# Attention beside a state-space scan on one core: input loaded in two token halves, first head group split by keys, rotation tables grown from 128 tokens

## The chip, the cores and the metric

The kernel runs on one core of a Trainium2 chip. The core has a matrix engine (TensorE: PE for its matmuls, PEld for its weight loads), a vector engine (VectorE, DVE), a scalar engine that evaluates functions (ScalarE, ACT), a general-purpose engine (GpSimd, POOL) and an engine that here only issues DMAs (SyncE, SP). Each engine runs its own list of instructions in order, and semaphores make one wait for another. The metric is the time of one execution on the device in microseconds (us), as the median of several runs.

## The reference

Two independent computations share the output, columns 0 to 639 and 640 to 1279 of a 2048-token sequence. The first (A) is a complex diagonal recurrence along the tokens, the second (B) is attention with 32 query heads that share one key and one value head of width 20.

```python
Lam_bar = exp(exp(log_dt) * Lam);  B_bar = ((Lam_bar - 1) / Lam)[:, None] * Bmat
Bu = einsum("bld,pd->blp", x, B_bar)
h = Lam_bar * h + Bu[:, t]                       # for t in 0..2047
y = 2 * einsum("bld,dp->bld", hseq, Cmat).real + x * Dskip

q = (x @ wq).reshape(1, 2048, 32, 20);  k = x @ wk;  v = x @ wv
p = softmax(einsum("bhqd,bkd->bhqk", q, k) * 20**-0.5)
b = einsum("bhqk,bkd->bhqd", p, v).reshape(1, 2048, 640) @ wo
out = concatenate([y, b], axis=-1)
```

## The kernel before, in words

The attention bounds the work. It is cut into 32 groups: 4 blocks of 512 queries times 8 groups of 4 heads. A group has 64 units, one for each of its 4 heads and each of 16 chunks of 128 keys; there are 2048 units. For a unit PE multiplies keys (`KT`) with queries (`QT`), which gives 128 x 512 scores in PSUM. Most units are then exponentiated on ACT, in tiles of three or two units (`ex_op`, P<-R, 128x1536 or 128x1024, line 1295). The rest ("D units") go to DVE, which makes an integer approximation of the exponential in one pass out of PSUM (line 1301) and three shifted copies from it in passes over several units (line 1307). PE multiplies the results with the values (`VP`) and sums a group in one PSUM bank, `PV`; a column of ones in `VP` gives the softmax denominators. When a group is complete, DVE copies `PV` to `OTr` (line 1343), from where it goes to memory, is normalized and multiplied with `wo`.

The scores need a bound that keeps the exponential in range. The row `mabs` holds the largest absolute key over all tokens for each of the 20 features; PE multiplies its table (`Mblk`) with the absolute queries and subtracts the product from the queries' scores by way of a constant key row (row 20 of each head in `KT`). This is called the guard. It needs the keys of all 2048 tokens before the first score.

The scan A turns the recurrence into a real one by rotating with cosine and sine tables `cs` of 5 x 512 columns, which `tables` builds in the set-up: three DVE passes and two ACT passes (lines 711 to 719) for each of 5 channel blocks. The DVE scan (line 957), products on POOL (line 945) and matmuls follow, spread over the whole run.

What sets the order: `setup` emits its instructions in the order in which they are written, then `main` runs a planner at build time. The planner has a list of threads (deques of operations), estimates when each operation could start, and appends the one that could start first, with small biases and some noise from a table of seeds, to its engine's list. So the order on every engine is fixed when the kernel is built, and an engine that waits holds up everything behind the wait. A thread named `rest` holds the end of the set-up (key copies, value products); while it is not empty, no PV product is offered, and not more than about half of the first group is filled.

In the set-up of before, SP issues six transposing DMAs for the attention's input `xbT` (four with 2048 tokens, the last channel block in two halves), PE forms all keys in four PSUM banks as the channel blocks arrive, DVE takes the largest absolute keys (line 574), ACT copies half of the keys to `KT` (line 565), and the guard follows.

Of the kernel before, what the change touches and what calls it, by code (L numbers as in the profile page):

```python
# [254 lines left out]
class _Kernel:  # L255
# [15 lines left out]
    SPIN = 1, 0, 5, 2  # L271
# [5 lines left out]
    SEEDS = (19, 1987, 2263, 3089, 4041, 5474, 6444, 7290, 8492, 9186, 10683, 11194, 12742, 13024, 14829,  # L277
# [33 lines left out]
    def alloc(self):  # L311
# [32 lines left out]
        self.sb("E1", [128, 4], BF16)  # L344
# [3 lines left out]
        self.tri = self.Pd[:].rearrange("p s u n -> p (s u n)").bitcast(FP32).rearrange("p (r n) -> p r n", n=512)  # L348
# [5 lines left out]
        self.wq_raw = self.P[:].rearrange("p s n -> p (s n)")[:, 18 * 512:18 * 512 + NC * 640].rearrange("p (c n) -> p c n", c=NC)  # L354
# [14 lines left out]
        self.sb("CGim", [128, NC, 640], BF16)  # L369
        self.sb("DiagD", [128, NC, 128], BF16)  # L370
        self.sb("sv", [128, 4, NC], FP32)
        self.sb("sc", [128, 24, NC], FP32)
        self.sb("ang", [128, 3, 4, NC], FP32)
        self.sb("rot", [128, 4, NC], FP32)
# [3 lines left out]
        self.sb("tm", [128, 8, 512], BF16)  # L378
        self.ctmp = self.tm[:].rearrange("p i n -> p (i n)").bitcast(FP32)[:, 1024:1664]
# [19 lines left out]
    def go(self, o):  # L399
        r, w = o.keys()  # L400
        occ = o.occ * self.pace(self.p.begin("pe", r, w, o.accum)) if o.eng == "pe" else o.occ
# [55 lines left out]
    def setup(self):  # L457
        t, NC, S = self.t, self.NC, self.S
        self.x_keys = [f"xbT{c}" for c in range(NC)] + [f"xbT{NC - 1}b"]
# [10 lines left out]
        go(self.dma(K.wk_raw, t["wk"].rearrange("(c p) n -> p c n", p=128), "wk", writes=["wk_raw"], kb=25, q="act"))  # L470
        go(self.dma(K.wq0, t["wq"][:, 0:80].rearrange("(c p) n -> p c n", p=128), "wq0", writes=["ostage0"], kb=100, q="act"))
        go(self.dma(K.wv_raw, t["wv"].rearrange("(c p) n -> p c n", p=128), "wv", writes=["wv_raw"], kb=25))
# [9 lines left out]

        pool(lambda e: e.memset(K.ident[:], 0.0), writes=["ident"])
# [5 lines left out]
        pool(lambda e: e.iota(K.iota_i, pattern=[[1, 512]], base=0, channel_multiplier=0), writes=["hh1"], occ=0.6)  # L489
        pool(lambda e: e.tensor_copy(K.iota_f, K.iota_i), reads=["hh1"], writes=["hh0"], occ=0.6)  # L490
        pool(lambda e: e.memset(K.wk4, 0.0), writes=["wk4"], occ=0.6)
# [4 lines left out]
        pool(lambda e: e.memset(K.wq0p, 0.0), writes=["ystage"], occ=0.6)  # L496
        dve(lambda e: e.memset(K.half[:], 1.0), writes=["half"], n=3)
        for j in range(4):
            dve(lambda e, j=j: e.memset(K.half[32 * j:32 * j + 32, 1 - j % 2:2 - j % 2], 0.0), ["half"], ["half"], n=1)

# [8 lines left out]
        pk = ["P7", "P8", "P9"]  # L509
        go(self.dma(K.wq_raw, t["wq"].rearrange("(c p) n -> p c n", p=128), "wq", writes=["wq_raw"] + pk, kb=800))  # L510
        pad = lambda x: x.rearrange("p c (j r) -> p c j r", r=32)[:, :, :, 0:20]
# [5 lines left out]
        for pat, base, cm, cmp in (([[0, 4], [1, 32]], -20, 0, ALU.is_equal),  # L517
# [4 lines left out]
                reads=mk, writes=mk, occ=0.4)  # L522
        pool(lambda e: e.memset(K.wq1[:], 0.0), writes=["wq1"], occ=0.6)
        pool(lambda e: e.memset(K.OTr[:, 1, :], 0.0), writes=["OTr1"], occ=0.6)

        self.tables(dve, act, {
            1: lambda: act(lambda e: e.activation(pad(K.wq0p), K.wq0.rearrange("p c (j r) -> p c j r", r=20), ACT.Copy),
                           ["ostage0", "ystage"], ["ystage"], n=400),
            3: turn})
        act(lambda e: e.activation(K.half[:, 2:3], K.half_pi[:], ACT.Exp), ["half_pi", "half"], ["half2"], n=1)  # L530


        banks = [(K.R[1], 0, "R1"), (K.R[1], 512, "R1b"), (K.BB, 0, "B0"), (K.BB, 512, "B1")]
        for bt, off, key in banks:
            go(self.mms([self.m1(bt[:, off:off + 512], K.selrow[:, :], K.onesrow[:, :], True, False)],
                        ["selrow", "onesrow"], [key], accum=True))
# [14 lines left out]
        for c in range(NC - 1):  # L551
            k_part(c, range(4))
            spin((0, 0, self.SPIN[0], 0)[c])
# [1015 lines left out]
```

## Time and profile before

| | |
|---|---|
| median of 3 runs | 756.54 us (755.94 to 757.65) |
| the profiled execution | 756.86 us, its span 755.1 us |
| ACT busy | 740.4 us (98%) |
| DVE busy | 711.0 us (94%) |
| PE busy | 699.2 us (93%) |
| POOL busy | 349.3 us (46%) |
| first exponential on ACT starts | 21.08 us |

The span reaches from the first to the last instruction. Busy times are unions: where two records of an engine overlap, the time counts once. A line of a timeline gives start, length, engine, source line, operation, output <- input, count, and in brackets the idle time before it with what ended it. A line of instruction groups gives the shapes, the count, busy time and the mean length of one in ns.

### The profile page before, as it was taken

How to read it: one execution, taken by the hardware profiler on the slowest of the kernel's cores; microseconds unless marked ns; L12 is line 12 of the kernel's file. 1: busy time of each engine (PE TensorE's matmuls, PEld its weight loads, DVE VectorE, ACT ScalarE, POOL GpSimd, SP SyncE). 2: the span in 40 equal slices, each digit the busy share in tenths (PEclk: the TensorE clock that was granted, in tenths of full speed). 3: DMA queues.
4: the chain of work that ended last, by engine and by line, in shares of the span. 5: the costliest groups of instructions: out<-in, count | busy, mean ns of one | idle time of the engine just before them, and what ended most of it. 6: DMA issues, size and time to landing. Idle time of an engine off the chain costs nothing.

```text
span 755.1 us, 22636 instructions
## 1 busy us (share of the span) xinstructions
PE 699.2 (93%) x9643; PEld 225.0 (30%) x9643; DVE 711.0 (94%) x1108; ACT 740.4 (98%) x712; POOL 349.3 (46%) x708
## 2 busy tenths in 40 slices
PE   5899987889999999999999999999999999989997
PEld 2222222222222333322223333222233332223334
DVE  6599999999998999999999899999999999999986
ACT  8999999999999999999999999999999999999995
POOL 5702344479975000287683201577722443882040
PEclk9799999999999999999899999999999999999999
DMA  9377301000020003200002002200000211000021
GB/s 191 66 128 155 68 16 50 8 25 16 4 58 16 33 19 76 68 11 16 15 10 70 26 25 77 60 8 18 8 25 20 69 42 40 1 16 17 21 62 37
DMA packets 61202, 31.89 MB, mean 42 GB/s; under 512 B 41510, under 2 KB 61102, under 8 KB 61102
## 3 DMA queue, kind: packets, MB, share of 16 engines
q1 hardware_dynamic: 59606, 30.14, 16.3%
q8 instruction: 77, 1.26, 0.7%
q10 hardware_dynamic: 1496, 0.30, 0.2%
q14 instruction: 23, 0.19, 0.1%
HBM read 9.21 MB, written 12.69 MB: 29 GB/s over the span
## 4 chain that ended last, share of the span: by engine, by line
ACT 63%; PE 21%; DVE 14%; issue 1%; POOL 1%; ACTq 0%; DVEq 0%
ACT P L1295 61%; PE R L448 7%; PE PV L448 7%; PE B L448 7%; DVE Pd L1307 5%; DVE Pd L1301 5%; DVE hh L957 2%; DVE tm L929 1%; ACT cs L719 0%; ACT KT L565 0%; DVE ostage L1089 0%; DVE OTr L1343 0%; ACT Pd L718 0%; DVE Qd L803 0%; ACTq L421 0%
## 5 line engine op out<-in xcount | busy, mean ns | idle before, releaser
L1295 ACT ACTIVATE P<-R 128x1024 bf16<-128x1024 f32 (+1 forms) x679 | 721.0, 1296 | 3.7 <-PE R L448 1.7
L448 PE MATMUL R<-QT,KT 32*128 32x512 bf16 (+1 forms) x1686 | 267.6, 389 | 36.6 <-ACT P L1295 26.6
L448 PE MATMUL PV<-Pd,VP 128*32 128x512 bf16 x1860 | 271.2, 385 | 4.0 <-DVE Pd L1307 1.7
L448 PE MATMUL PV<-P,VP 128*32 128x512 bf16 x1583 | 265.5, 389 | 0.4
L1301 DVE TENSOR_SCALAR Pd<-B 128x512 int16<-128x512 f32 x362 | 243.8, 681 | 15.4 <-PE B L448 13.1
L1307 DVE TENSOR_SCALAR Pd<-Pd 128x1536 int16<-128x1536 int16 (+3 forms) x356 | 250.0, 709 | 2.8
L945 POOL TENSOR_TENSOR tm<-hh,cs 128x128 bf16<-128x128 f32 x320 | 161.1, 528 | 162.9 <-DVE hh L957 153.5
L448 PEld LDWEIGHTS R<-QT,KT 32*128 32x128 bf16 (+1 forms) x1686 | 67.0, 91 | 294.2 <-ACT P L1295 264.5
L448 PE MATMUL B<-QT,KT 32*128 32x512 bf16 x362 | 140.0, 387 | 0.0
L945 POOL TENSOR_TENSOR W<-tm 128x128 bf16<-128x128 bf16 x160 | 79.9, 523 | 37.2 <-PE B L448 33.0
L448 PEld LDWEIGHTS PV<-Pd,VP 128*32 128x32 bf16 x1860 | 65.7, 94 | 70.3 <-issue 41.9
L448 PEld LDWEIGHTS PV<-P,VP 128*32 128x32 bf16 x1583 | 63.6, 94 | 51.3 <-issue 39.6
L1301 DVE TENSOR_SCALAR Pd<-R 128x512 int16<-128x512 f32 x103 | 69.9, 678 | 1.3 <-PE R L448 1.0
L1039 POOL TENSOR_TENSOR OTd<-OTd,rwide 128x128 bf16<-128x128 bf16 x80 | 34.2, 455 | 72.9 <-DMA OTd<-o_rows 71.0
L886 POOL TENSOR_SCALAR tm<-W,sc 128x128 f32<-128x128 bf16 x40 | 30.0, 765 | 63.9 <-DMA W<-in_A_C_im_dram 26.6
L929 DVE TENSOR_TENSOR tm<-B,cs 128x1024 bf16<-128x1024 f32 x40 | 48.6, 1214 | 1.1 <-PE B L448 0.9
L448 PE MATMUL B<-CGre,W 128*32 128x384 bf16 (+1 forms) x640 | 47.7, 304 | 0.0
L448 PE MATMUL B<-CGim,W 128*32 128x384 bf16 (+1 forms) x640 | 46.9, 299 | 0.0
L957 DVE TENSOR_TENSOR_SCAN hh<-sc,hini,B 128x512 f32<-128x512 f32 x30 | 38.0, 1270 | 0.0
L448 PEld LDWEIGHTS B<-QT,KT 32*128 32x128 bf16 x362 | 32.8, 91 | 0.5 <-DVE ystage L990 0.3
L448 PE MATMUL B<-xaT,BTre 128*32 128x512 bf16 x400 | 32.3, 383 | 0.5 <-DVE hh L957 0.3
L448 PE MATMUL B<-xaT,BTim 128*32 128x512 bf16 x400 | 32.3, 395 | 0.5 <-DVE tm L929 0.2
(153 smaller groups left out, 438.4 us busy)
## 6 DMA issues: line engine op xcount, KB each, us to landing
o_rows<-OTr SPq DMA_DIRECT2D x32, 128.0 KB, 1.7
QT<-q_rows SPq DMA_DIRECT2D x30, 128.0 KB, 2.2
q_rows<-Qd SPq DMA_DIRECT2D x16, 160.0 KB, 2.9
OTd<-o_rows SPq DMA_DIRECT2D x16, 160.0 KB, 3.3
out_dram<-ystage SPq DMA_DIRECT2D x16, 160.0 KB, 1.8
out_dram<-ostage SPq DMA_DIRECT2D x12, 160.0 KB, 1.8
P<-in_B_wq_dram SPq DMA_DIRECT2D x1, 800.0 KB, 5.2
WO<-in_B_wo_dram SPq DMA_DIRECT2D x4, 200.0 KB, 3.6
```

The lines of the kernel that those rows point to most:

```text
L448: ins = e.matmul(o() if callable(o) else o, lhsT=l, rhs=r, start=st, stop=sp, skip_group_check=True, **kw)
L886: pool(lambda e, y=y, c=c, gy=gy, i=i: e.tensor_scalar(K.ctmp[:, i:i + 128], y[:, i:i + 128], sc[:, gy, c:c + 1], None, op0=ALU.mult), key ...
L929: dve(lambda e, k=k, h=h: e.tensor_tensor(K.tm[:, 2 * k:2 * k + 2, :], bass.AP(tensor=K.BB, offset=512 * int(h.key[1]), ap=[[512 * self.BA ...
L945: put(lambda e, c0=c0, end=end: e.tensor_tensor(out[:, c0:end], a[:, c0:end], b[:, c0:end], op), reads, [writes + h], n, gate=None if i el ...
L957: dve(lambda e, ri=ri, ini=ini, h=h: e.tensor_tensor_scan(K.hh[:, ri, :], dec, h.T[:, :], ini, ALU.mult, ALU.add), ["sc", None, "hini"], [ ...
L1039: ops.append(Op("pool", lambda e, c=c, m=m: e.tensor_tensor(K.OTd[:, m, c], K.OTd[:, m, c], K.rwide[:, c], ALU.mult), rw + [f"OTe{dd}" for ...
L1295: return Op("act", lambda e: e.activation(dst, K.R[n % 2][:, 0:512 * size], ACT.Exp, scale=self.exp_scale), [f"R{n % 2}"] + ["R0c"] * (siz ...
L1301: return Op("dve", lambda e: e.tensor_scalar(K.Pd[:, 0, u, :], K.B[x][:, :], self.d_off, 0.0, op0=ALU.add, op1=ALU.max), [key], [f"Pd{u}_0 ...
L1307: return Op("dve", lambda e: e.tensor_scalar(K.Pd[:, i:i + n, a:b, :].rearrange("p s u n -> p s (u n)"), K.Pd[:, 0:n, a:b, :].rearrange("p ...
```

## The change

Four things are changed together, and a new table of seeds comes with them.

1. **Two token halves.** `xbT` is loaded by ten transposing DMAs of 1024 tokens, first all five channel blocks of tokens 0 to 1023, then those of 1024 to 2047. In `setup` PE forms the keys of the first half only, in the two banks `B0` and `B1`. The second half's keys are in `rest`, and the value products, one operation for each half and channel block (8 small matmuls), in a new thread `vals`.
2. **First head group split by keys.** Group 0 becomes two blocks: block -1 over key chunks 0 to 7 and block 0 over key chunks 8 to 15, with 32 units each. Block -1 uses queries `QT3` whose guard comes from the first half's keys. `rest` then forms the guard of all keys, the queries `QT0` that use it (PE adds the difference of the two guards to `QT3`, then one DVE copy), and a factor `frac`, the exponential of the difference of the two guards (8 matmuls with `E1`, one ACT pass of 128x512). When block -1 is complete, DVE multiplies its `PV` with the factor into `early`; when block 0 is complete, DVE adds `early` to its `PV`. `frac` and `early` lie in `OTd`, which is not used that early.
3. **Tables grown.** `tables` builds cosine and sine for tokens 0 to 127 of all five channel blocks in one go (four DVE passes and one ACT pass over 128x640, one ACT pass over 128x1280). The other 384 columns are rotations of them: for each of 5 channel blocks, 3 steps and 2 tables, one POOL product (`growth`, a multiplication with a per-partition scalar, 128x128 in 32-bit floats) and one DVE operation that multiplies and adds, 30 of each. The DVE ones are in a thread `grow`. No D unit is taken for block -1, nor while `rest` or `grow` is not empty.
4. **Set-up in the scheduler.** The threads `rest`, `vals`, `loads` (inputs of the scan), `grow` and `guard` (the small DMAs of `mabs`) are all given to the planner. The raw `wq` moves from the ring `P` to `CGre`. The load of `wv` moves from SP to ACT's queue. PE's filler products, which add zeros to `PV` where PE would be idle, read `xbT` in place of `cs`.

The orders of the instructions around three places follow, before and then after. First, ACT from the last table of the set-up to the first exponential; `sv` are per-channel constants, `sc` the decay, `Qabs` the absolute queries of the guard.

```order
L701 ACTIVATE rot<-ang 128x20
L718 ACTIVATE Pd<-Pd,quarter 128x512
L719 ACTIVATE cs<-Pd,half_pi 128x1024
L530 ACT_TABLE_LOAD
L530 ACTIVATE half<-half_pi 128x1
L579 ACTIVATE sv<-R 128x5 x2
L581 ACTIVATE Qabs<-PV 128x512
L565 ACTIVATE KT<-R,half 128x512 x4
L594 ACTIVATE sc<-sc 128x5
L1295 ACTIVATE P<-R 128x1536
```

```order
L521 ACTIVATE WO<-WO 128x5x20 x4
L758 ACTIVATE Pd<-Pd,quarter 128x640
L759 ACTIVATE tm<-Pd,half_pi 128x1280
L743 ACTIVATE rot<-ang 128x50
L573 ACTIVATE sv<-R 128x5 x2
L574 ACT_TABLE_LOAD
L574 ACTIVATE half<-half_pi 128x1
L577 ACTIVATE sc<-sc 128x5
L600 ACTIVATE Qabs<-R 128x512
L586 ACTIVATE KT<-B,half 128x512 x4
L1362 ACTIVATE P<-R 128x1536
```

The two table passes for each of five channel blocks have become two passes in all, and the constants `sv` and the decay stand ahead of the guard's queries.

Second, DVE from the first queries `QT` onward.

```order
L786 TENSOR_SCALAR QT<-PV 128x512
L596 TENSOR_TENSOR mabs<-mabs 128x1
L569 TENSOR_SCALAR KT<-B,half 128x512 x4
L602 MEMSET VP 128x1024
L603 MEMSET VP 128x16 x4
L605 TENSOR_SCALAR VP<-PV 128x16x20 x4
```

```order
L846 TENSOR_SCALAR QT<-R 128x512
L763 CAST cs<-tm 128x10x128
L781 SCALAR_TENSOR_TENSOR cs<-tm,rot,Pd 128x128 x19
L632 TENSOR_SCALAR VP<-PV 128x16x20 x4
L617 TENSOR_TENSOR mabs<-mabs 128x1
L638 TENSOR_REDUCE mabs<-B 128x1
L617 TENSOR_TENSOR mabs<-mabs 128x1 x2
L590 TENSOR_SCALAR KT<-B,half 128x512 x2
L643 TENSOR_SCALAR Mblk<-Pd,mabs 128x128
L781 SCALAR_TENSOR_TENSOR cs<-tm,rot,Pd 128x128 x4
L630 CAST QT<-B 128x512
```

A cast and 19 of the 30 growth operations now stand between the first queries and the values `VP`, and the second half's guard behind those. On POOL the 30 products of the growth stand directly behind the product for the decay:

```order
L593 TENSOR_TENSOR sc<-sc,sv 128x5
L611 COPY wqd<-P 128x640 x5
L614 TENSOR_SCALAR nident<-ident 128x128
L650 MEMSET Md 128x160
L652 AFFINE_SELECT Md<-Md 128x160 x4
```

```order
L576 TENSOR_TENSOR sc<-sc,sv 128x5
L779 TENSOR_SCALAR Pd<-tm,rot 128x128 x30
L688 MEMSET Md 128x160
L690 AFFINE_SELECT Md<-Md 128x160 x4
L656 COPY wqd<-CGre 128x640 x5
```

The copies `wqd`, the weights from which the queries of groups 2 to 7 are made, have moved behind the 30 products.

Third, PE after the value products, in the stretch in which ACT works on its first tiles (R are the tiles of scores).

```order
L448 MATMUL PV<-WO,xbT 128x20 x20
L448 MATMUL R<-QT,KT 128x512 x7
L448 MATMUL PV<-P,VP 32x512 x8
L448 MATMUL R<-QT,KT 128x512 x3
L448 MATMUL PV<-P,VP 32x512 x4
```

```order
L453 MATMUL R<-QT,KT 128x512 x2
L453 MATMUL PV<-P,VP 32x512 x4
L453 MATMUL B<-QT,ident 128x512
L453 MATMUL B<-Qabs,Mblk 128x512
L453 MATMUL R<-QT,KT 128x512 x3
L453 MATMUL PV<-xbT,VP 32x512 x4
L453 MATMUL R<-QT,KT 128x512 x2
L453 MATMUL PV<-P,VP 32x512 x4
L453 MATMUL B<-QT,E 32x512 x8
```

PE now forms the second queries (`B<-QT,ident` and `B<-Qabs,Mblk`) ahead of the scores of the eleventh tile, and the factor's exponent (`B<-QT,E`) ahead of those of the thirteenth.

Over the whole program ACT has 445 exponentials of 1024 and 232 of 1536 columns where it had 454 and 225, DVE has 462 D units where it had 465, and PE has 160 filler products where it had 100.

The diff, cut to its core:

```diff
-        for c in range(NC):
-            for t0, n, key in (((0, S, f"xbT{c}"),) if c < NC - 1 else ((0, S // 2, f"xbT{c}"), (S // 2, S // 2, f"xbT{c}b"))):
-                go(self.dma(K.xbT[:, c, t0:t0 + n], t["xb"][0, t0:t0 + n, 128 * c:128 * (c + 1)], key, writes=[key], tr=True,
-                            kb=n // 4))
+        for i, h in enumerate("ab"):
+            for c in range(NC):
+                key, t0 = f"xbT{c}{h}", 1024 * i
+                go(self.dma(K.xbT[:, c, t0:t0 + 1024], t["xb"][0, t0:t0 + 1024, 128 * c:128 * (c + 1)], key, writes=[key],
+                            tr=True, kb=256))
...
+        go(ones(0))
+        go(ones(1))
+        for c in range(NC):
+            for tb in range(2):
+                go(k_mm(c, tb))
+            if c < 2:
+                spin(self.SPIN[0])
+            elif c == 2:
+                for o in blk[:3]:
+                    go(o)
+                go(self.mms([self.m1(K.R[1][:, 0:10], K.vecD, K.ident[0:10, 0:10], True, True)], ["ident", "veclre", "vecdsk"], ["R1"]))
...
+        self.rest = deque([
+            ones(2), ones(3), *(k_mm(c, tb) for c in range(NC) for tb in (2, 3)),
+            small(3, 0, 1, ALU.max, ["mabs0", "mabs1"]),
+            Op("dve", lambda e: e.tensor_reduce(out=mcol(2), in_=K.BB[:, 0:1024], axis=AX.X, op=ALU.max,
+                                                apply_absolute_value=True), ["B0", "B1"], ["mabs2"], occ=dve_t(1024)),
+            top,
+            small(3, 4, 3, ALU.subtract, ["mabs4", "mabs3"]),
+            *copy("dve", 2),
+            Op("dve", lambda e: e.tensor_scalar(K.Mblk[:], K.mask, mcol(3), self.c1, op0=ALU.mult, op1=ALU.mult), mk + ["mabs3"], ["Mblk"],
+               occ=dve_t(128)),
+            *again, *last,
...
+            self.mms(diff, ["E1", "QT0", f"QT{self.QRING - 1}"], ["B0"], kind="C"),
+            Op("act", lambda e: e.activation(K.frac, K.B[0][:, :], ACT.Exp, scale=self.exp_scale), ["B0"], self.frac_keys,
+               occ=act_t(512), lat=0.12),
...
+    def growth(self, pool):
+        K, NC, grow = self, self.NC, self.grow
         for c in range(NC):
+            for k in (1, 2, 3):
+                for i in range(2):
+                    m = 2 * (3 * c + k - 1) + i
+                    tmp, tk = K.flat[:, 4608 + 128 * m:4736 + 128 * m], f"gt{m}"
+                    s, co = K.rot[:, 2 * k, c:c + 1], K.rot[:, 2 * k + 1, c:c + 1]
+                    pool(lambda e, c=c, i=i, s=s, tmp=tmp: e.tensor_scalar(tmp, K.base[:, 1 - i, c, :], s, None, op0=ALU.mult),
+                         self.base_keys + ["rot"], [tk], 0.385)
+                    grow.append(Op("dve", lambda e, c=c, i=i, co=co, tmp=tmp, k=k: e.scalar_tensor_tensor(
+                        out=K.cs[:, c, i, 128 * k:128 * k + 128], in0=K.base[:, i, c, :], scalar=co, in1=tmp, op0=ALU.mult,
+                        op1=(ALU.subtract, ALU.add)[i]), self.base_keys + ["rot", tk] + self.row_keys(9 + m // 4),
+                        [f"cs{c}{i}{k}"], occ=dve_t(128)))
...
-        qt_done = self.qt_done = {0}
+        qt_done = self.qt_done = {-1}
+        half_kc = self.NKC // 2
+        blocks = [range(half_kc, self.NKC)] + [range(self.NKC)] * (NG - 1) + [range(half_kc)]
...
-            if not (g > 0 or taken[g] >= 24) or d_group(g) is None:
+            if g < 0 or rest or self.grow or d_group(g) is None:
                 return False
...
+            if g < 0:
+                return Op("dve", lambda e: e.tensor_tensor(K.early, K.PV[:, :], K.frac, ALU.mult), ["PV"] + K.frac_keys, K.early_keys,
+                          occ=dve_t(512))
+            if g == 0:
+                return Op("dve", lambda e: e.tensor_tensor(K.OTr[:, sl, :], K.PV[:, :], K.early, ALU.add), ["PV"] + K.early_keys,
+                          [f"OTr{sl}"], occ=dve_t(512))
```

More of the change, by code (lines that the diff above doesn't have):

```diff
@@ L585, in setup @@
                 go(o)
-        last = bass.AP(tensor=K.mabs, offset=1, ap=[[5, 128], [0, 128]])
-        dve(lambda e: e.scalar_tensor_tensor(out=K.Mblk[:], in0=last, scalar=K.mabs[:, 0:1], in1=K.mask, op0=ALU.max,
+        dve(lambda e: e.scalar_tensor_tensor(out=K.Mblk[:], in0=wide(1), scalar=mcol(0), in1=K.mask, op0=ALU.max,
                                              op1=ALU.mult), mk + ["mabs0", "mabs1"], ["Mblk"], n=128)
+        spin(self.SPIN[1])
+        va = [self.v_part(0, c) for c in range(NC)]
@@ new lines, in setup @@
+        top = small(4, 2, 3, ALU.max, ["mabs2", "mabs3"])
+        top.done = lambda: self.max_done.add(0)
+        last = list(copy("dve", 3))
+        last[-1].done = lambda: self.qt_done.add(0)
+        self.max_done = set()
+        diff = [self.m1(K.B[0][32 * j:32 * j + 32, :], bass.AP(tensor=K.E1, offset=4 * i + j, ap=[[8, 128], [0, 32]]),
+                        K.QT[:, r, :], i == 0, i == 1, (0, 32 * j), 4) for i, r in ((0, 0), (1, self.QRING - 1)) for j in range(4)]
+        q1, q2 = K.QT[:, self.QRING - 1, :], K.QT[:, 0, :]
@@ L1352, in main @@
             cand = []
-            if half and not any(x[1][0] == half[0][1][0] for x in dunits) and taken[half[0][1][0]] > self.DLAST:
+            if half and not any(x[1][0] == half[0][1][0] for x in dunits) and late(half[0][1][0]):
                 shifts.extend((tuple(half), x) for x in self.PASSES)
@@ L1361, in main @@
             t_fill = None
-            early = bool(rest) and any(self.NKC - len(x) >= 8 for x in left[0])
-            if cur["fill"] < cur["act"] + 2 and any(x < 64 for x in taken) and not early:
+            if cur["fill"] < cur["act"] + 2 and taken != size_of:
                 n = cur["fill"]
-                g = next(i for i in range(NG) if taken[i] < 64)
+                g = next(i for i in groups if taken[i] < size_of[i])
                 if g in qt_done:
```

319 lines of the change are left out of this document (167 added, 152 removed), and 8 rows, old and new, of the table SEEDS.

## The prediction

> **What bounds the kernel now.** I read the page's busy times and chain first, then the windows and waits of ACT, then the timeline of the set-up, since the change is made there.
>
> ```profile
> span 755.1 us, 22636 instructions
> ACT 63%; PE 21%; DVE 14%; issue 1%; POOL 1%; ACTq 0%; DVEq 0%
> 21.00:100.00 79.00, 74.39 (x938) 22.24 (x938) 70.41 (x123) 78.13 (x75) 28.59 (x57) 0.94 0.54 101
> 100.00:745.00 645.00, 606.17 (x8484) 193.86 (x8482) 624.13 (x952) 642.14 (x608) 308.53 (x622) 0.99 0.11 30
> 745.00:755.10 10.10, 6.32 (x190) 4.52 (x180) 3.28 (x6) 2.27 (x3) 0.00 (x0) 0.93 0.20 68
> L1295 ACT ACTIVATE P<-R 128x1024 bf16<-128x1024 f32 (+1 forms) x679 | 721.0, 1296 | 3.7 <-PE R L448 1.7
> ...
> L1295 ACT ACTIVATE P<-R 128x1024 bf16<-128x1024 f32 x454 | 473.7, 1152 | 1.9 <-PE B L448 0.9 <-PE R L448 0.6
> L1295 ACT ACTIVATE P<-R 128x1536 bf16<-128x1536 f32 x225 | 357.2, 1588 | 1.8 <-PE R L448 1.1 <-PE B L448 0.4
> ```
>
> In a window's row the fourth busy time is ACT's: it is idle for 0.87 us from 21 to 100 and for 2.86 us from 100 to 745. So between the first exponential and the tail ACT is full, and the time is: start of the first exponential, plus ACT's work, plus a few us of idle, plus a tail of ten. The chain's 14% on DVE warn that DVE (624.13 of 645, 96.8%) is nearly as full. Before the first exponential the timeline of ACT reads:
>
> ```profile
> 1.68 0.41 ACTq L421 DMA_DIRECT2D WO<-in_B_wk_dram  x1
> ...
> 4.36 1.28 ACT L503 ACT_TABLE_LOAD   x1
> 5.96 1.24 ACT L507 ACTIVATE WO<-WO 128x100 bf16<-128x100 bf16 x4
> ...
> 14.81 0.70 ACT L718 ACTIVATE Pd<-Pd,quarter 128x512 f32<-128x512 f32 x1
> 15.55 1.15 ACT L719 ACTIVATE cs<-Pd,half_pi 128x1024 bf16<-128x1024 f32 x1
> 16.72 1.28 ACT L530 ACT_TABLE_LOAD   x1
> 18.01 0.20 ACT L530 ACTIVATE half<-half_pi 128x1 f32<-128x1 f32 x1
> 18.12 0.22 ACT L579 ACTIVATE sv<-R 128x5 f32<-128x5 f32 x2
> 18.23 0.60 ACT L581 ACTIVATE Qabs<-PV 128x512 f32<-128x512 f32 x1
> 18.71 2.44 ACT L565 ACTIVATE KT<-R,half 128x512 bf16<-128x512 f32 x4
> 20.99 0.25 ACT L594 ACTIVATE sc<-sc 128x5 f32<-128x5 f32 x1
> 21.08 2.41 ACT L1295 ACTIVATE P<-R 128x1536 bf16<-128x1536 f32 x2
> ```
>
> ACT hardly pauses: the ten table passes (7 to 16.7) hold up the first exponential as much as the data.
>
> **The change, part by part.** *Half the input.* The last two transposes of before have the new size:
>
> ```profile
> 0.79 12.46 SPq L419 DMA_TRANSPOSE xbT<-in_B_x_dram  x6
> L419 SPq DMA_TRANSPOSE xbT<-in_B_x_dram x2: 1299/1300/1301, 10.6 to 11.9; - x2
> DMA to landing us min/median/max: 3.7/3.8/3.9
> 8.94 1.03 PE L448 MATMUL R<-xbT,WO 128*128 128x512 bf16 x2
> 9.76 1.06 PE L448 MATMUL B<-xbT,WO 128*128 128x512 bf16 x2
> 13.57 0.81 PE L448 MATMUL R<-xbT,WO 128*128 128x512 bf16 x3
> 14.22 0.59 PE L448 MATMUL B<-xbT,WO 128*128 128x512 bf16 x2
> ```
>
> At 1.3 us an issue and 3.8 to land, the fifth half lands at 0.8 + 4 x 1.3 + 3.8 = 9.8, the tenth at 16.3. PE starts when ACT has copied `wk` (7.2 before; 7.6 now, since the DMA of `wv` adds 0.4, as that of `wk` took, to ACT's queue). A product takes 0.41 cold (9.76 - 8.94 for two) and 0.22 ((14.22 - 13.57)/3) from 4.6 us after the first. Eight key and spin products cold end at 11.0, three query products at 12.2, so `sv` is on ACT at 12.4 and the last key product at 13.6. The data are not the limit; the second half arrives behind cover (needed at about 22, as PE's products of it are spread among the first tiles).
>
> *ACT's set-up.* From `sv` at 12.4: 0.3, table load 1.3, two small ones 0.45, `Qabs` 0.6, four key copies 2.44: first exponential at 17.5. PE and DVE are in step: maxima of 512 (half of the 1.21 below, twice) to 14.9, `Mblk` 0.35, product 0.4, `QT` 0.69, scores 0.6: 17.2. Gain 21.1 - 17.5 = **-3.6**.
>
> *More on ACT.* Before: 2 x 454 + 3 x 225 = 1583 units in 721.0 us of busy time (the first of the groups of line 1295 above, where overlapping records count once), 0.455 each. After: 2 x 445 + 3 x 232 = 1586, **+1.4**. The factor is one pass of 512, between 0.6 (`Qabs`, and a fourth of the key copies) and 0.7 (line 718): **+0.6**.
>
> *The growth.* This is the risk, because 19 of DVE's operations, each behind a POOL product, stand ahead of `VP`, and PE's first PV product stands ahead of the scores of the eighth tile.
>
> ```profile
> L886 POOL TENSOR_SCALAR tm<-W,sc x40: 600/607/1423, 65.3 to 137.9; 128x128 f32<-128x128 bf16 x40
> L886 POOL TENSOR_SCALAR tm<-W,sc 128x128 f32<-128x128 bf16 x40 | 30.0, 765 | 63.9 <-DMA W<-in_A_C_im_dram 26.6 <-DVE CGre L888 22.6 <-DVE CGim L888 13.9
> L945 POOL TENSOR_TENSOR tm<-hh,cs x320: 419/429/1498, 159.6 to 678.5; 128x128 bf16<-128x128 f32 x160
> 17.29 1.21 DVE L574 TENSOR_REDUCE mabs<-B 128x1 f32<-128x1024 f32 x1
> 18.61 0.35 DVE L587 SCALAR_TENSOR_TENSOR Mblk<-mabs,Pd 128x128 bf16<-128x128 f32 x1
> 19.53 0.69 DVE L786 TENSOR_SCALAR QT<-PV 128x512 bf16<-128x512 f32 x1 [0.57 <-PE PV L448]
> 20.14 0.43 DVE L596 TENSOR_TENSOR mabs<-mabs 128x1 f32<-128x1 f32 x1
> 20.49 2.71 DVE L569 TENSOR_SCALAR KT<-B,half 128x512 bf16<-128x512 f32 x4
> 26.18 1.68 DVE L605 TENSOR_SCALAR VP<-PV 128x320 bf16<-128x320 f32 x4 [1.13 <-PE PV L448]
> L605 DVE TENSOR_SCALAR VP<-PV 128x320 bf16<-128x320 f32 x4 | 1.7, 483 | 1.1 <-PE PV L448 1.1
> 32.85 0.69 DVE L1301 TENSOR_SCALAR Pd<-B 128x512 int16<-128x512 f32 x1 [2.10 <-PE B L448]
> 19.22 6.54 POOL L611 COPY wqd<-P 128x640 bf16<-128x640 bf16 x5 [0.66 <-DMA P<-in_B_wq_dram]
> 26.74 1.81 POOL L652 TENSOR_SCALAR_AFFINE_SELECT Md<-Md 128x160 bf16<-128x160 bf16 x4
> ```
>
> DVE: `QT` ends at 16.55, the cast of 1280 columns adds 1.4 (estimate: twice the 0.69 of 512 would be 1.7 for 1280, the maxima's 1.21 for 1024 give 1.5), to 18.0. A growth operation is at most 0.35 (`Mblk`, same shape); four in a row overlap (line 605: 1.68 for four of 0.483, 0.06 less each), so I take 0.27. If POOL keeps up, the 19th ends at 18.0 + 19 x 0.27 = 23.1. POOL starts its 30 behind the decay's product at 12.8, and keeps up if one costs no more than (23.1 - 0.3 - 12.8)/19 = 0.53. No row has this operation: two inputs with 32-bit in cost 0.429, a scalar multiplication of other types 0.607. I take the middle, 0.52, and keep both ends; 0.607 is the nearer by operation, 0.429 by input type.
>
> Then DVE needs 1.7 (`VP`), 1.2 (maximum), 0.7 (three tiny ones), 1.4 (two key copies), 0.25: `Mblk` at 28.4. PE makes the second queries by 29.0 and, behind them, the scores of the eleventh tile by 29.55. ACT's ten tiles before it take 5 x (5 x 0.455) = 11.4 from 17.5, to 28.8. Stall **+0.75**. The factor's product comes with the thirteenth tile, after 30.1, and adds nothing. The 0.87 us that ACT idled there before are replaced: **-0.87**.
>
> *Moved behind cover.* `wqd` starts behind the 30 products at 12.8 + 15.6 + 2 = 30.4 and ends at 37 (was 25.8); PE meets it only at ACT's seventeenth tile, about 36, behind `wqd`'s third copy at 34.4. If POOL is slower, this is what is late next. D units start behind the growth, near 32; the first of before is at 32.9. The 30 additions on DVE (8.1) and the cast replace table passes that ran before the first exponential, but larger shift batches and three D units fewer give back as much. The merge is two DVE passes in place of one copy at the same width. 60 more filler products run where PE waits. SP's ten issues take 13 us as six took 12.5. Zero each.
>
> *Sum* on the profiled execution, 756.86 (0.32 above the median of the runs): 756.86 - 3.6 + 1.4 + 0.6 + 0.75 - 0.87 = 755.14, on the median's scale **754.8**. A change of 0.2% (1.5 us) is about what a measurement of this kernel can tell from none, so this lies just on the faster side of 755.0.
>
> **Rivals.** *POOL at 0.607.* The 19th product is done at 24.3, DVE 24.6, everything behind it 1.5 later: 756.3, within 0.2%. For it: the same kind of operation with a scalar from memory. Against: its input is of another type.
>
> *POOL slower still, because DVE is in its way.* Line 886's mean is 0.765 against its median of 0.607: its products beside DVE are stretched. At 0.765 the 19th is done at 27.3, DVE 27.6; the stall grows by 4.5, and the time is 759.3. It ends slower (above 758.05) once the stall grows by 3.25, that is from 0.70 on. Against: DVE is mostly waiting in that stretch. [...]
>
> *An earlier start that is worth nothing.* DVE, at 96.8% from 100 to 745, could be what ends last. Its D units start no earlier, so ACT runs dry later by what it gained: 756.54 + 1.4 + 0.6 = 758.5. Against: ACT's waits from 100 to 745 come to 2.86 us only; for it: the chain runs through DVE for 14%.
>
> **How the numbers follow.** Forecast (faster or on the edge) 0.47: 0.42 faster, 0.05 same. POOL at 0.607: 0.15 (0.13 same, 0.02 slower). POOL stretched: 0.22 slower. Earlier start worth nothing: 0.16 (0.06 same, since DVE need only limit in part, 0.10 slower). So faster 0.42, same 0.24, slower 0.34. The likeliest case alone spans 751.9 (also the 2.86 us of idle gone) to 756.3 (POOL at its nearest row). The range goes from 751.9 to the stretched rival, 759.3.
>
> **What would show it.** First exponential at 17 to 18; ten tiles without a gap, then a wait of ACT under 1 us for scores behind `B<-QT,ident`; POOL's 30 products at 0.43 to 0.53; the first PV product near 24; idle of ACT after 100 of 3 us. Wrong if the products exceed 0.6, if ACT's table passes wait for DVE beyond 8.5, if PE is still cold at 12 (six products at 0.41: +1.1), or if ACT's idle after 100 exceeds 6.

## The result and the profile after

The changed kernel takes **761.98 us** (median of 5 runs, 759.66 to 763.04) against 756.54 for the kernel before in the same five rounds (754.99 to 757.65): the ratio is 1.007, with a 95% interval of 1.0048 to 1.0091. The change makes the kernel slower by 0.7%. The forecast was 754.8, with a range up to 759.3.

The profiled execution of after took 761.37 us, its span is 759.5. The page's row of the exponentials and ACT's windows, then ACT's timeline from the first exponential on (start, length, engine, line, operation, and in brackets the idle time before it):

```profile
L1362 ACT ACTIVATE P<-R 128x1024 bf16<-128x1024 f32 (+1 forms) x677 | 722.3, 1297 | 11.4 <-PE R L453 7.2
...
17.00:100.00 83.00, 73.28 (x875) 22.20 (x875) 77.66 (x136) 72.38 (x68) 35.38 (x64) 0.92 0.53 104
100.00:750.00 650.00, 611.02 (x8602) 196.91 (x8602) 626.30 (x952) 649.25 (x611) 321.19 (x637) 1.00 0.11 30
...
16.76 8.23 ACT L1362 ACTIVATE P<-R 128x1536 bf16<-128x1536 f32 x7
28.18 1.02 ACT L1362 ACTIVATE P<-R 128x1024 bf16<-128x1024 f32 x1 [3.19 <-PE R L453]
29.70 2.37 ACT L1362 ACTIVATE P<-R 128x1536 bf16<-128x1536 f32 x2 [0.50 <-PE R L453]
...
39.85 2.36 ACT L1362 ACTIVATE P<-R 128x1536 bf16<-128x1536 f32 x2 [2.42 <-PE B L453]
44.95 1.02 ACT L1362 ACTIVATE P<-R 128x1024 bf16<-128x1024 f32 x1 [2.73 <-PE R L453]
```

The first exponential starts at 16.76 instead of 21.08: 4.3 us are won. Then 11.4 us of idle time stand before exponentials where before had 3.7, and nearly all of it lies between 25 and 50 us: in three large pieces of 3.19, 2.42 and 2.73 and some of half a us. From 100 us on ACT idles 0.75 us in 650, less than before (2.86 in 645).

So the account of the profiled executions, 756.86 to 761.37, is: -4.3 (start), +1.3 (exponentials 722.3 in place of 721.0), +0.6 (the factor's pass), +7.7 (idle), -0.5 (the tail after the last exponential: 8.7 in place of 9.3 from its end to the span's end). That makes +4.8, and +4.5 was measured.

Where do the 7.7 us come from? POOL and DVE in the same stretch of after:

```profile
12.55 19.69 POOL L779 TENSOR_SCALAR Pd<-tm,rot 128x128 f32<-128x128 f32 x30
34.34 6.76 POOL L656 COPY wqd<-CGre 128x640 bf16<-128x640 bf16 x5
...
17.53 4.69 DVE L781 SCALAR_TENSOR_TENSOR cs<-tm,rot,Pd 128x128 bf16<-128x128 f32 x14
22.73 1.51 DVE L781 SCALAR_TENSOR_TENSOR cs<-tm,rot,Pd 128x128 bf16<-128x128 f32 x3 [0.50 <-POOL Pd L779]
24.74 1.03 DVE L781 SCALAR_TENSOR_TENSOR cs<-tm,rot,Pd 128x128 bf16<-128x128 f32 x2 [0.50 <-POOL Pd L779]
25.69 1.67 DVE L632 TENSOR_SCALAR VP<-PV 128x320 bf16<-128x320 f32 x4
...
34.10 3.06 DVE L781 SCALAR_TENSOR_TENSOR cs<-tm,rot,Pd 128x128 bf16<-128x128 f32 x3
37.09 0.35 DVE L651 COPY wq<-CGre 128x400 bf16<-128x400 bf16 x1
37.36 4.27 DVE L781 SCALAR_TENSOR_TENSOR cs<-tm,rot,Pd 128x128 bf16<-128x128 f32 x4
41.56 0.68 DVE L842 TENSOR_SCALAR Qabs<-B 128x512 int32<-128x512 int32 x1
```

Two things stand out. POOL's 30 products took 0.656 us each (19.69/30), DVE caught up with them after 14, and `VP` came at 25.69, for which PE's first PV product waited. And the growth's operations that cost DVE 0.335 us each at first (4.69/14) cost 1.0 us each after 34 us (3.06/3, 4.27/4), just while POOL makes its five copies of `wqd`. Behind them stand the copy of `wq` for the queries of group 1 and the absolute queries `Qabs`. PE waits for `VP`, for that copy and for `Qabs`, and ACT waits for PE. PE's timeline of after:

```profile
27.42 0.40 PE L453 MATMUL PV<-P,VP 128*32 128x512 bf16 x4 [3.92 <-DVE VP L632]
37.59 1.67 PE L453 MATMUL B<-xbT,wq 128*32 128x512 bf16 x20 [2.13 <-DVE wq L651]
42.29 0.62 PE L453 MATMUL B<-Qabs,Mblk 128*32 128x512 bf16 x4 [1.40 <-DVE Qabs L842]
```

### The profile page after: what moved, and what is told of

Its sections match the earlier page's. It is cut to its first block, busy times and chain, and to the rows that moved or that the text cites. A ratio compares the mean times of both kernels' runs of the same rounds, so it can differ in the third digit from the quotient of the medians.

```text
span 759.5 us, 22797 instructions
## 1 busy us (share of the span) xinstructions
PE 700.3 (92%) x9703; PEld 227.5 (30%) x9705; DVE 716.0 (94%) x1117; ACT 735.1 (97%) x702; POOL 369.4 (49%) x739
## 3 DMA queue, kind: packets, MB, share of 16 engines
q8 instruction: 77, 1.26, 0.7%
## 4 chain that ended last, share of the span: by engine, by line
ACT 78%; PE 12%; DVE 7%; POOL 2%; issue 1%; ACTq 0%
ACT P L1362 77%; PE B L453 5%; PE R L453 4%; PE PV L453 3%; DVE Pd L1374 2%; POOL Pd L779 2%; DVE Pd L1368 2%; DVE cs L781 1%; DVE tm L991 1%; DVE hh L1019 1%; ACTq L426 0%; DVE KT L590 0%; DVE VP L632 0%; ACT L515 0%; DVE mabs L638 0%
## 5 line engine op out<-in xcount | busy, mean ns | idle before, releaser
L1362 ACT ACTIVATE P<-R 128x1024 bf16<-128x1024 f32 (+1 forms) x677 | 722.3, 1297 | 11.4 <-PE R L453 7.2
L453 PE MATMUL PV<-P,VP 128*32 128x512 bf16 x1586 | 270.7, 389 | 5.1 <-DVE VP L632 3.9
L1374 DVE TENSOR_SCALAR Pd<-Pd 128x1536 int16<-128x1536 int16 (+3 forms) x338 | 243.4, 727 | 2.8
L1007 POOL TENSOR_TENSOR tm<-hh,cs 128x128 bf16<-128x128 f32 x320 | 163.9, 535 | 156.9 <-DVE hh L1019 140.7
L1007 POOL TENSOR_TENSOR W<-tm 128x128 bf16<-128x128 bf16 x160 | 81.6, 533 | 36.0 <-PE B L453 31.8
L1368 DVE TENSOR_SCALAR Pd<-R 128x512 int16<-128x512 f32 x98 | 66.8, 682 | 2.3 <-PE R L453 2.0
L947 POOL TENSOR_SCALAR tm<-W,sc 128x128 f32<-128x128 bf16 x40 | 33.9, 860 | 55.8 <-DMA W<-in_A_C_im_dram 20.7
L453 PE MATMUL B<-xbT,wqd 128*32 128x512 bf16 x400 | 30.8, 400 | 0.0
```

The source lines that it names most:

```text
L453: ins = e.matmul(o() if callable(o) else o, lhsT=l, rhs=r, start=st, stop=sp, skip_group_check=True, **kw)
L947: pool(lambda e, y=y, c=c, gy=gy, i=i: e.tensor_scalar(K.ctmp[:, i:i + 128], y[:, i:i + 128], sc[:, gy, c:c + 1], None, op0=ALU.mult), key ...
L1007: put(lambda e, c0=c0, end=end: e.tensor_tensor(out[:, c0:end], a[:, c0:end], b[:, c0:end], op), reads, [writes + h], n, gate=None if i el ...
L1362: return Op("act", lambda e: e.activation(dst, K.R[n % 2][:, 0:512 * size], ACT.Exp, scale=self.exp_scale), [f"R{n % 2}"] + ["R0c"] * (siz ...
L1368: return Op("dve", lambda e: e.tensor_scalar(K.Pd[:, 0, u, :], K.B[x][:, :], self.d_off, 0.0, op0=ALU.add, op1=ALU.max), [key], [f"Pd{u}_0 ...
L1374: return Op("dve", lambda e: e.tensor_scalar(K.Pd[:, i:i + n, a:b, :].rearrange("p s u n -> p s (u n)"), K.Pd[:, 0:n, a:b, :].rearrange("p ...
```

## The experiments

All but one are the changed kernel with every engine's order of instructions kept, so that the planner's choices don't differ between the runs; only the named instructions have another form, and two kernels have a fill on VectorE near 10.5 us besides. Each was timed in rounds with the kernel before; ratios are to it. The kernel before itself took 756.39 to 757.06 in these rounds, so a difference between two runs of different rounds is uncertain by some tenths of a us. **Theory P** is that the growth is late because of POOL: its products are slow, and its copies slow DVE down. The rivals: DVE has too many growth operations in any case (D), or `wqd` itself is late for the dense queries (W).

**No products.**

```diff
-pool(e.tensor_scalar(tmp, K.base[:, 1 - i, c, :], s, None, op0=ALU.mult), ...)
+pool(e.memset(tmp[:, 0:8], 0.0), ...)
-grow: scalar_tensor_tensor(..., in1=tmp, ...)
+grow: scalar_tensor_tensor(..., in1=self.lane(tmp), ...)     # one column, step 0
```

> The changed kernel with the order of all instructions as it is, but each of GpSimd's 30 products of the table growth is replaced by a fill of 8 columns, and the DVE operation behind it reads one column of it over and over. Left out: the second product of each rotation, so the tables are wrong beyond token 128. Theory P (the growth is late because a GpSimd product took 0.656 us, and everything that stands behind the growth on DVE and on GpSimd is late with it): the growth's DVE operations run at 0.33 us each without a gap, the copies of wqd on GpSimd start some 12 us earlier than at 34.3, ScalarE's idle time before exponentials falls from 11.4 to 2 or 3 us, and the time from 762 to 752 to 755. Rival D (the 30 DVE operations themselves are too many, whatever GpSimd does): the idle time stays above 8 us and the time above 759.

Measured: **754.27** us, ratio 0.9956 (0.9937 to 0.9975). ACT's idle time before exponentials is 4.9 us, more than the 2 or 3 foreseen, `VP` is at 23.32, and the copies of `wqd` start at 21.82, when `wq` lands. The growth's operations have a median of 0.347 us, none above 0.37, and the first 19 follow each other every 0.267 us (5.07/19 below). 7.7 us below the changed kernel: rival D falls, since the 30 DVE operations are all still there.

The copies meet other DVE work in this run:

```profile
21.82 2.77 POOL L656 COPY wqd<-CGre 128x640 bf16<-128x640 bf16 x1 [3.98 <-DMA CGre<-in_B_wq_dram]
...
18.34 5.07 DVE L785 SCALAR_TENSOR_TENSOR cs<-tm,rot,Pd 128x128 bf16<-128x128 f32 x19
...
24.91 0.97 DVE L617 TENSOR_TENSOR mabs<-mabs 128x1 f32<-128x1 f32 x1
```

The first copy starts among the growth's operations, and here it is the copy that waits: it takes 2.77 us and ends 1.18 behind the last of them (24.59 against 23.41), while they keep their pace. So POOL is not always the one that gets ahead; what decides it was not tried, and here the growth's second input is a single column. An operation on `mabs`, one column wide with two inputs in SBUF, took 0.97 us beside a copy, against 0.20 in after (at 27.28). ACT's longest wait of this run, 2.65 us at 31.75, is for what stands behind these operations (`Mblk`, and PE's second queries).

**No growth.**

```diff
+dve(e.memset(K.cs[:], 0.0), ...)          # near 10.5 us, where DVE idles
-grow: out=K.cs[:, c, i, 128 * k:128 * k + 128], in0=K.base[:, i, c, :]
+grow: out=K.cs[:, c, i, 128 * k:128 * k + 8], in0=K.base[:, i, c, 0:8]
```

> As the run without products, and the DVE operations of the growth are 8 columns wide as well, so the growth costs next to nothing on both engines while its instructions and its order stay. Left out: the tables beyond token 128. It gives the price of the whole growth. Theory P: 1 or 2 us below the run without products, 751 to 754, with less than 2 us of idle time before exponentials. If the time stays above 759, the lost time near 28 to 46 us is not the growth's at all, and theory P falls.

Measured: **753.94** us, ratio 0.9962 (0.9949 to 0.9975), with 2.7 us of idle time before exponentials, a little more than foreseen. DVE's whole share of the growth is worth 0.3 us in place of the 1 or 2 foreseen, within what runs differ by. What the growth costs, it costs through POOL.

**Products as products of two tensors.**

```diff
-e.tensor_scalar(tmp, K.base[:, 1 - i, c, :], s, None, op0=ALU.mult)
+e.tensor_tensor(tmp, K.base[:, 1 - i, c, :], bass.AP(tensor=K.rot,
+    offset=2 * k * NC + c, ap=[[10 * NC, 128], [0, 128]]), ALU.mult)
```

> The changed kernel with the order as it is; GpSimd's 30 products are written as a product of two tensors, the second of them the factor of each partition repeated, in place of a product with a per-partition scalar. Everything is computed. Theory P: if the product of two tensors costs what line 945 of before did (0.43 us), 30 of them end 6 to 7 us earlier, the copies of wqd start at 28 instead of 34, and 4 to 8 of the 11.4 us of idle time go: 754 to 758. If the form makes no difference (0.65 us), the time stays at 762. Rival D: the products get faster and the time stays above 760 all the same.

Measured: **759.73** us, ratio 1.0026 (1.0015 to 1.0038). The price was foreseen, the time was not: only 2.3 us came back. The timelines of POOL and DVE in this run:

```profile
13.41 12.62 POOL L779 TENSOR_TENSOR Pd<-tm,rot 128x128 f32<-128x128 f32 x30
28.11 6.67 POOL L656 COPY wqd<-CGre 128x640 bf16<-128x640 bf16 x5
...
18.28 8.15 DVE L782 SCALAR_TENSOR_TENSOR cs<-tm,rot,Pd 128x128 bf16<-128x128 f32 x19
26.36 1.67 DVE L632 TENSOR_SCALAR VP<-PV 128x320 bf16<-128x320 f32 x4
...
32.18 3.41 DVE L782 SCALAR_TENSOR_TENSOR cs<-tm,rot,Pd 128x128 bf16<-128x128 f32 x4
```

POOL needs 0.42 us a product (12.62/30), and DVE, which never waits for one now, needs 0.43 for each of its own (8.15/19), in place of 0.335 in after and 0.267 without products. DVE has fallen into step with POOL, and `VP` starts 8.08 us after the first growth operation, against 8.16 in after. The copies, 6 us earlier, now meet four other growth operations (0.85 us each). So there is more to POOL than its price.

**Short copies of `wqd`.**

```diff
+dve(e.memset(K.wqd[:], 0.0), ...)         # near 10.5 us, where DVE idles
-pool(e.tensor_copy(K.wqd[:, c, :] ..., K.wq_raw[:, c, :] ...))     # 640 columns
+pool(e.tensor_copy(K.wqd[:, c, 0:32], K.wq_raw[:, c, 0:32]))
```

> The changed kernel with the order as it is; GpSimd's five copies that permute wq to wqd copy 32 columns in place of 640, and a fill of wqd by VectorE stands in its idle time near 10.5 us. Left out: the permuted weights of the dense queries. Theory P with its second half (the growth's last DVE operations were stretched from 0.33 to about 1.0 us because GpSimd's copies ran beside them, and so the copy of wq for the queries of group 1 and Qabs were late): the DVE operations between 34 and 42 us come back to 0.35 us each, ScalarE's waits of 2.42 and 2.73 us near 40 and 45 shrink below 1 us together, the 3.19 us near 28 stay, and the time is 757 to 758. Rival W (the dense queries' matmuls wait for wqd itself): the same time, but the DVE operations stay at 1.0 us. Rival D: the time stays above 760.

Measured: **755.99** us, ratio 0.9983 (0.9970 to 0.9996). The waits near 40 and 45 are gone, one of 3.31 near 28 is left, and the time is 1 us better than foreseen: 6.0 us of the loss hang on the copies, though the products take as long as in after. The growth's last seven operations, in after and in this run (count, and duration in ns as least, median, most):

```profile
L781 DVE SCALAR_TENSOR_TENSOR cs<-tm,rot,Pd x7: 415/1395/1422, 34.1 to 41.2; 128x128 bf16<-128x128 f32 x7
```

```profile
L781 DVE SCALAR_TENSOR_TENSOR cs<-tm,rot,Pd x7: 343/346/347, 35.8 to 37.6; 128x128 bf16<-128x128 f32 x7
```

**No copies, and copies that nobody reads.** The last run leaves open whether the copies stretch DVE, or whether earlier `wqd` does the good. So `wq` is loaded into `wqd`'s place, and PE reads the permuted columns from there. In one kernel the copies become fills of 8 columns; in the other POOL still copies, into a tile that is not yet in use.

```diff
-self.wq_raw = self.CGre[:]
+self.wq_raw = self.wqd[:]
-K.wqd[:, c, 128 * m:128 * m + 128]
+K.wqd[:, c, :].rearrange("p (h d) -> p d h", d=20)[:, 4 * m:4 * m + 4, :]
-pool(e.tensor_copy(K.wqd[:, c, :].rearrange("p (d h) -> p d h", h=32), K.wq_raw ...))
+pool(e.memset(K.CGre[:, c, 0:8], 0.0))                                        # no copies
+pool(e.tensor_copy(K.CGre[:, c, :].rearrange("p (d h) -> p d h", h=32), K.wq_raw ...)) # idle copies
```

> The changed kernel with the order as it is, without the five copies that permute wq: wq lands in wqd's own place and the dense queries' matmuls read their 32 columns from it 20 apart. In place of each copy GpSimd fills 8 columns of CGre. Everything is computed. If GpSimd's copies beside VectorE's growth are the larger part of the loss, as the run with short copies says, the growth's DVE operations take 0.35 us each and the time is 755 to 757. If reading weights 20 columns apart costs TensorE something, it shows in the weight loads of wqd and the time is above 757.

> As the run with wq read in place, but GpSimd still makes the five copies of 640 columns, at their old place in its order, from wqd to CGre, where nobody reads them. Nothing on the chip waits for these copies but what GpSimd does behind them. Theory P in its second half (the copies stretch VectorE's two-input operations): the growth's DVE operations between 34 and 42 us are at 1.0 us again, the waits of 2.4 and 2.7 us are back, and the time is 761 to 763. Rival W (wqd was late): the time stays at 755 to 757.

Measured: **755.48** us without copies (ratio 0.9992, 0.9977 to 1.0006), **761.40** with copies that nobody reads (1.0068, 1.0049 to 1.0087). The second is the loss of the changed kernel, its waits of 2.58 and 2.66 us included. Rival W falls, and the cause is shown: POOL's copies beside DVE's growth. Reading the weights 20 columns apart is not free for the weight loads (a median of 139 ns in place of 96 for the 400 of `wqd`), but they lie beside matmuls, whose median is 379 ns in both, and the time doesn't show it.

How the copies do it is seen when single records of after are taken from its timeline, a copy and the growth operation beside it:

```profile
34.34 1.35 POOL L656 COPY wqd<-CGre 128x640 bf16<-128x640 bf16 x1
35.65 1.37 POOL L656 COPY wqd<-CGre 128x640 bf16<-128x640 bf16 x1
39.70 1.41 POOL L656 COPY wqd<-CGre 128x640 bf16<-128x640 bf16 x1
...
34.10 0.41 DVE L781 SCALAR_TENSOR_TENSOR cs<-tm,rot,Pd 128x128 bf16<-128x128 f32 x1
35.77 1.40 DVE L781 SCALAR_TENSOR_TENSOR cs<-tm,rot,Pd 128x128 bf16<-128x128 f32 x1
39.83 1.42 DVE L781 SCALAR_TENSOR_TENSOR cs<-tm,rot,Pd 128x128 bf16<-128x128 f32 x1
```

The operation that starts before the first copy takes 0.41. Those that start 0.12 or 0.13 us behind a copy end 0.14 or 0.15 us behind its end (35.65 + 1.37 = 37.02 against 37.17; 39.70 + 1.41 = 41.11 against 41.25). DVE gets through one growth operation for each of these copies. The copies themselves are hardly slower for it (1.34 to 1.41 us against 1.33 in before, where no growth ran beside them), and the copy of `wq` on DVE at 37.09, which has one input in SBUF, took its 0.35 in the middle of them.

**Plain copies, and fills.** To see what in a copy does it, the idle copies are made without the permutation, and then replaced by fills of the same size.

```diff
-pool(e.tensor_copy(K.CGre[:, c, :].rearrange("p (d h) -> p d h", h=32), K.wq_raw ...))
+pool(e.tensor_copy(K.CGre[:, c, :], K.wqd[:, c, :]))                          # plain copies
+pool(e.memset(K.CGre[:, c, :], 0.0))                                          # fills
```

> As the run with copies that nobody reads, but the five copies on GpSimd are contiguous on both sides: 640 columns to 640 columns, without the permutation. It asks what in the copies stretches VectorE's growth. If any copy by GpSimd does while it runs, the growth's DVE operations beside it are at 1.0 us again, and the time follows from how long the five copies last: 759 to 762 if a copy takes 1.2 us or more, 757 to 759 if it takes half of that. If only the strided side does it, the DVE operations take 0.35 us and the time is 755 to 757.

> As the run with copies that nobody reads, but the five copies are fills of the same 640 columns: GpSimd writes as much and reads nothing. If it is GpSimd's reading that stretches VectorE, as its own fills elsewhere would say, the growth's DVE operations take 0.35 us and the time is 755 to 757; if its writing does too, some of them are at 1.0 us and the time is 757 to 760, since a fill of 640 columns took 0.66 us in the profile of before against 1.33 for a copy.

Measured: **758.13** us with plain copies (ratio 1.0019, 1.0006 to 1.0033), **755.56** with fills (0.9982, 0.9968 to 0.9996). POOL and DVE in the run with plain copies, then in the run with fills:

```profile
35.16 3.60 POOL L656 COPY CGre<-wqd 128x640 bf16<-128x640 bf16 x5
...
35.88 2.30 DVE L781 SCALAR_TENSOR_TENSOR cs<-tm,rot,Pd 128x128 bf16<-128x128 f32 x3
38.38 1.44 DVE L781 SCALAR_TENSOR_TENSOR cs<-tm,rot,Pd 128x128 bf16<-128x128 f32 x4
```

```profile
34.77 3.03 POOL L656 MEMSET CGre<- 128x640 bf16 x5
...
34.79 1.26 DVE L646 TENSOR_SCALAR Mblk<-Pd,mabs 128x128 bf16<-128x128 f32 x1
34.98 1.07 DVE L781 SCALAR_TENSOR_TENSOR cs<-tm,rot,Pd 128x128 bf16<-128x128 f32 x3
35.77 0.35 DVE L651 COPY wq<-wqd 128x400 bf16<-128x400 bf16 x1
36.04 1.13 DVE L781 SCALAR_TENSOR_TENSOR cs<-tm,rot,Pd 128x128 bf16<-128x128 f32 x4
```

A plain copy takes 0.72 us (3.60/5), half of a permuted one, and beside it a growth operation takes 0.77 (2.30/3): again one for each copy. Beside fills of 0.61 us the growth's operations start every 0.26 us (three from 34.98 to 35.77), and the last four keep 0.28 each (1.13/4). The first three all end at 36.05, together with the `Mblk` ahead of them, a product with one input in SBUF that took 1.26 us here and 0.28 in after (at 33.91); what held that one up was not tried. The time shows no loss: 755.56 with fills, 755.48 without copies. So the growth is stretched beside POOL's copies, which read and write (0.77 us each beside plain ones), and keeps its pace beside fills, which only write (0.26 to 0.28), and the loss grows with the length of a copy: 5.9 us with permuted copies (761.40 against 755.48), 2.6 with plain ones (758.13 against 755.56). It is not so in every meeting: the first copy of the run without products took 2.77 us while the growth kept its pace (0.267 us each), and beside POOL's products with a scalar, which read too, a growth operation took 0.307 to 0.335 us (below).

**Both causes taken away.**

```diff
 # wq in place, no copies, as above, and
-pool(e.tensor_scalar(tmp, K.base[:, 1 - i, c, :], s, None, op0=ALU.mult))
+pool(e.tensor_tensor(tmp, K.base[:, 1 - i, c, :], <s repeated>, ALU.mult) if m < 11 else
+     e.tensor_scalar(tmp, K.base[:, 1 - i, c, :], s, None, op0=ALU.mult))
```

> As the run with wq read in place, and GpSimd's first 11 products, which end before VectorE's growth begins, are written as products of two tensors (0.42 us each), the other 19 stay as they are (0.656 us). Everything is computed. Both causes of the loss are then taken away: no wait of VectorE for a product, VP near 24.5 us, 753.5 to 755.5, below the kernel before by about 2 us. If only one of them counted, 756 to 757.

Measured: **753.45** us, ratio **0.9960** (0.9945 to 0.9975): it computes everything and is faster than both kernels. ACT's idle row and the timelines of POOL and DVE:

```profile
L1364 ACT ACTIVATE P<-R 128x1024 bf16<-128x1024 f32 (+1 forms) x677 | 722.1, 1294 | 2.9 <-PE R L453 2.2
...
13.36 4.47 POOL L779 TENSOR_TENSOR Pd<-tm,rot 128x128 f32<-128x128 f32 x11
17.93 12.80 POOL L781 TENSOR_SCALAR Pd<-tm,rot 128x128 f32<-128x128 f32 x19
...
18.59 5.83 DVE L783 SCALAR_TENSOR_TENSOR cs<-tm,rot,Pd 128x128 bf16<-128x128 f32 x19
24.34 1.67 DVE L632 TENSOR_SCALAR VP<-PV 128x320 bf16<-128x320 f32 x4
```

The cheap form is used while DVE has not begun, the other one, beside which DVE isn't slowed much (0.307 us, 5.83/19, against 0.267 with no products), from then on. DVE waits for no product, and `VP` starts 5.75 us after its first growth operation, against 8.16 in after (17.53 to 25.69).

**The kernel before without its copies.**

```diff
-self.wq_raw = self.P[:] ...
+self.wq_raw, self.wq_old = self.wqd[:], self.P[:] ...
-pool(e.tensor_copy(K.wqd[:, c, :] ..., K.wq_raw[:, c, :] ...))
+pool(e.memset(K.wq_old[:, c, 0:8], 0.0))
```

> The kernel before with wq read in place and its five copies on GpSimd replaced by fills of 8 columns, the order as it is. Everything is computed. In before the copies ran at 19 to 26 us, beside no growth on VectorE, so they cost nothing there: 756 to 757.5, the same as before. If it falls below 755.5, the copies cost the kernel before something too, and what the changed kernel gains by reading wq in place is not the change's.

Measured: **755.97** us, ratio 0.9999 (0.9987 to 1.0010). In before the copies cost nothing that the time shows. What the last version gains is the change's own gain, freed of what it lost beside the copies.

Against the changed kernel's 761.98 the runs give: faster products alone -2.3, no stretch by the copies alone -6.0 to -6.5, both -7.7 (with products left out) to -8.5 (with everything computed). The first two add up to -8.3 to -8.8, so within what runs differ by they stand side by side.

## Why the prediction was wrong

**Start: right.** 17.5 was forecast, and the profiled executions of these kernels show 16.8 to 18.0. The spread is PE's: in after the three query products at 11.15 took 0.81 us together, in the last version, at 11.30, they took 1.49, and the first exponential came 1.06 later (17.82). The prediction had them slow, near the latter's pace. What decides it was not tried. Two steps on the way don't add up as written: by its own terms `QT` ends at 16.34 and not at 16.55, and 1280 columns at the rate of 512 are two and a half times 0.69, not twice. Neither moves the forecast by more than 0.2 us.

**More work on ACT, the factor: right.** +1.3 and 0.60 were measured against +1.4 and +0.6.

**"The growth", POOL's product: mis-sized.** It took the middle, 0.52, between a product of two tensors and one with a scalar. The row that was nearest by operation was the right one: alone, before DVE begins, a product takes 0.602, against that row's 0.607. Beside DVE's growth it takes 0.659, and 0.656 is the mean pitch of all 30, above the 0.6 that the prediction had named as a sign of being wrong. With it `VP` came at 25.69 instead of 23.1, and the stall was not 0.75 but 3.9 us (3.19, 0.50 and, at 32.32, 0.25). The growth's own operation was taken at 0.27, which is what it costs with no products beside it (0.267); in after the first 14 cost 0.335, which is a smaller part of it.

**"Moved behind cover ... Zero each": the step that failed.** The prediction placed the copies rightly, behind the products (30.4 to 37; measured 34.3 to 41.1, late with the products), and saw that PE would meet `wqd` late enough. It asked who waits for the copies, and the answer, nobody, holds: PE's dense products at 42.9 did not wait. It did not ask what runs beside them. The last seven growth operations, priced at 0.27 with the rest, cost 1.0 us each, `Qabs` came at 41.56, the first D unit at 42.16 instead of near 32, and ACT lost 6.2 us (2.42, 2.73, 0.49 and 0.59). The runs with idle copies and without copies put this at 5.9 us (761.40 - 755.48).

**"Idle of ACT after 100 of 3 us": better than forecast.** 3 us were expected to stay, 0.75 did.

**The rival that came nearest** was the stretched POOL, with 759.3: POOL and DVE did slow each other in the growth, with the larger loss the other way about. POOL was stretched from 0.602 to 0.659, not to 0.765, and DVE, by POOL's copies, threefold. The row that gave the 0.765 shows another meeting: of the 40 products of line 886, the 15 longest (0.75 us and more) each overlap a shift pass `Pd<-Pd` of line 1307 by 0.28 us or more, and the other 25 (0.65 us at most) by less; such a pass has one input in SBUF and a growth operation two, so the row's 0.765 was measured beside other DVE work than the growth. The rival's place (19 operations ahead of `VP`) gave 3.9 of the 10.2 us that ACT idled between 25 and 50 us, and the range, which ended there, was 2.7 us too short. The rival of an earlier start that is worth nothing fell: with the growth's losses taken away, the start's gain arrives at the end. The forecast without its stall, 754.8 - 0.75 = 754.0, is near what the runs without growth and with both causes away measured: 753.94 and 753.45. That is partly luck: ACT still waited 1.4 us between 26 and 36 us in these runs (0.92 and 0.47; 0.79 and 0.66), and 0.8 us of idle time after 100 us in place of 3 made up for it.

## What to carry to other kernels

When work is moved on GpSimd, look not only for who waits for it but for what VectorE does beside it: beside GpSimd's copies and products of two tensors the growth's operations, which have two inputs in SBUF, advanced by one for each GpSimd instruction (0.43 us beside products of 0.42), so a 1.4 us copy turned a 0.34 us operation into a 1.4 us one. Once, in the run without products, it was the copy that waited instead (2.77 us). Put such copies beside VectorE work that reads PSUM, as in before (1.33 us each; 755.97 us without them against 756.39), make them short (755.99 against 761.98), or do without them (755.48). A single input in SBUF doesn't make VectorE's work harmless in every form: the products of line 886 that lay beside the shift passes of before took up to 1.42 us in place of 0.6. For the price of an operation that no row shows, the row of the same operation with other types was nearer here (0.607 for a measured 0.602) than the row of another operation with the same input type (0.429).

## What the runs showed of the hardware

- On GpSimd a product of a 128x128 fp32 tile with a scalar of each partition takes 0.60 us, and the same product with the scalar repeated as a second tensor takes 0.40: the form with one tensor input is the slower. From after (before DVE's growth begins, then beside it) and from the run with products of two tensors (before):

```profile
L779 POOL TENSOR_SCALAR Pd<-tm,rot x8: 602/602/628, 12.6 to 16.9; 128x128 f32<-128x128 f32 x8
...
L779 POOL TENSOR_SCALAR Pd<-tm,rot x7: 597/659/944, 17.6 to 21.9; 128x128 f32<-128x128 f32 x7
```

```profile
L779 POOL TENSOR_TENSOR Pd<-tm,rot x12: 393/399/533, 13.4 to 18.0; 128x128 f32<-128x128 f32 x12
```

- The two forms treat VectorE differently. Beside the two-tensor form DVE's growth fell to its pace (0.43 us each, one for one). Beside the scalar form, which reads SBUF as well, DVE needed 0.307 us each in the last version and 0.335 in after, where it also waited, about two operations for each product (0.267 with no products), and the product grew by a tenth, from 0.602 to 0.659. One for one doesn't describe that pair; why the two forms differ was not tried.
- A copy on GpSimd that permutes 640 bf16 columns (read 20 apart) takes 1.35 us, a contiguous one 0.72.
